# A fused attention and two expert layers: the reciprocal of the row sums taken before they are spread, and each group's value matmuls queued as one block

## The chip, the cores and the metric

The kernel runs on one core of one Trainium2 chip. The metric is the device time of one execution in microseconds (us); the figure for a kernel is the median of its timed runs. For the kernel before it is 1182.77 us over 3 runs, which lie between 1182.54 and 1185.65 us.

Five engines work side by side, each with its own in-order queue: TensorE (PE in the rows, with its weight loads as PEld), VectorE (DVE), ScalarE (ACT), GpSimd (POOL) and SyncE (SP, which here only issues DMAs).

## The reference, cut to what matters

```python
scores = scale * np.matmul(q_rot, k_rot.transpose(0, 1, 3, 2))      # B=2, H=8, S=576, D=64
scores = scores - np.max(scores, axis=-1, keepdims=True)
attn = np.exp(scores)
attn = attn / (np.sum(attn, axis=-1, keepdims=True) + 1e-09)
x = np.matmul(attn, v)                   # then laid out as (B*S, H*D) = (1152, 512)
x = ((x @ w1) * (x @ w2)) @ w3 @ w_out   # first layer, d_ff = 1024
P = sinkhorn(exp(x @ w_gate - max))      # 8 rounds over 1152 tokens x 8 experts
out = sum(P[:, e:e+1] * (np.maximum(x @ mw1[e], 0.0) @ mw2[e]) for e in range(8))
```

q and k are rotated before the scores (rotary embedding). Everything is float32.

## The kernel before, in words

The program has two stages. **Attention** comes first and is followed by the two matmul layers, which are not touched by the change (they begin with `branch`, L646, and end with `project`, L829).

Attention goes over 8 pairs of heads (`n`, two heads `j` per pair, 64 rows of the contraction each). The 576 queries of a pair are five tiles of 128 rows (the fifth, `MIX`, holds the last 64 queries of both heads), and the tiles form two groups (`TILES`): group 0 has tiles 0 and 1 (256 queries per head), group 1 has tiles 2, 3 and 4 (320 queries per head). Per tile and head:

- `scores` (L327, L340; `mixed_scores` L345, L363 for the fifth tile): matmuls into the PSUM tile `s`, two buffers.
- `row_max` (L370, VectorE) and `exponentials` (L374, ScalarE), which also leaves the row sum in one column of `sm`.
- `transposes` (L388, L391, L394, TensorE) of the exponentials `e` into the PSUM tile `t`, and `moved` (L407, VectorE or ScalarE) from there into `et0` or `et1`, which have one buffer each.

Per group:

- `norm_sums` (L411, ScalarE) adds 1e-9 to the 4 or 5 sums per row.
- `norm_rows` (L418, VectorE) takes the reciprocal of the sums, read 64 times each through a broadcast, so that it writes 128x256 or 128x320 elements into `rb`.
- `norm_columns` (L424, L427, TensorE) transposes `rb`; `norm_moved` (L432, ScalarE) copies the result out of PSUM into `r`.
- `values` (L440, TensorE): five parts `t` = 0 to 4, each a pair of matmuls of V against `et` that write the two 64-row halves of the PSUM tile `x` (one buffer, pool psX). One such matmul shows as two rows of the trace, so a group is 20 rows.
- `x_scale` (L448, VectorE) multiplies `x` with `r` into `xs` and frees `x`; `x_hi` (L459, ScalarE) and `x_lo` (L463, GpSimd or VectorE) split it into two parts.

Between these stand steps for the next layers: 24 weight units of 128x512 (`wide_steps` L565: L183, L188, L191, L196, L201, L204 on ScalarE, VectorE and GpSimd) and the product of two weight matrices (`w34_product`, L231 to L233, on TensorE). Rotating q and k of later pairs is on GpSimd (L272, L276, L292).

The order of all of it is worked out before the kernel is emitted by `Plan` (L52). Every step has a cost in us on its engine, a rank, the steps it needs, the buffers it takes and the buffers it frees. `Plan.order` moves a clock forward; whenever an engine is free it picks, of the steps that could start now, the one with the lowest rank. The order in which the steps are picked is the order in which they stand in the engines' queues. The plan assumes 0.36 us (256 elements) and 0.43 us (320 elements) for `norm_rows` by `on_dve`, and adds `TURN` = 0.1 us whenever TensorE goes from a `paired` step (`values`) to another or back:

```python
if e == "pe":
    d += self.TURN * (paired != was_paired)
    was_paired = paired
```

In the plan the value steps of group 0 have a rank of t + 23 and those of group 1 of t + 34 (t grows by 18 per pair): they come behind the scores of the next pair where both could start. Each of the five parts is a step of its own, so other TensorE work may be queued between two parts. Where the plan leaves TensorE idle early on, matmuls of an identity (L615) are put in to fill the time.

Of the kernel before, what the change touches and what calls it, by code (L numbers as in the profile page):

```python
# [18 lines left out]
P = 128  # L19
B, H, S, D = 2, 8, 576, 64  # L20
# [7 lines left out]
MID = NBLK // 2  # L28
SPAD = 640
NQ = NBLK // 2 + 1  # L30
MIX = NQ - 1
SF = 2 * P
HS = S // 2
G0, G1 = 256, S - 256
HD = P // 2
TILES = (0, 1), (2, 3, 4)
CN = 320, 256
# [83 lines left out]
def attention_two_moes(ctx: ExitStack, tc: tile.TileContext, rope, qk, v, mw12, mw3t, mwo, wg, ew1, ew2, out):  # L121
# [7 lines left out]
    pe, act, dve, pool, sp = nc.tensor, nc.scalar, nc.vector, nc.gpsimd, nc.sync  # L129
# [12 lines left out]
    def three(ps, terms):  # L142
# [15 lines left out]
    psS, psT, psX, psW = (  # L158
        aps.enter_context(tc.tile_pool(name=n, bufs=k, space=PSUM)) for n, k in (("psS", 2), ("psT", 2), ("psX", 1), ("psW", 1))
    )  # L160
# [89 lines left out]
    V = [att_p.tile([P, NBLK + 1, D], F32, name=f"v{i}") for i in range(2)]  # L250
# [7 lines left out]
    raw, K, st = {}, {}, {}  # L258
# [37 lines left out]
    def spread_q(n, j, x):  # L296
# [5 lines left out]
        else:  # L302
            sp.dma_start(dst[:, : MIX * P], src[:, : MIX * P])
            sp.dma_start(dst[:, MIX * P + HD :], src[:, MIX * P :])

# [7 lines left out]
    def half(j):  # L313
        return slice(j * D, (j + 1) * D)

    def group(i):

        return (0, i, i * P) if i < 2 else (1, i - 2, i * P - G0)
# [26 lines left out]
    def mixed_scores(n):  # L345
# [5 lines left out]
        for j in range(2):  # L351
# [6 lines left out]

            pieces = [(0, 0, 0, HS), (1, 0, HS, HS)] if j == 0 else [(0, 0, HD, HS), (1, 0, HD + HS, HS - HD), (1, HS - HD, 0, HD)]
            terms += [(q, k, pieces) for q, k in new]  # L360
# [18 lines left out]
    def transposes(n, i, part):  # L379
# [12 lines left out]
        if part:  # L392
            for j in range(2):
                pe.matmul(ps[half(j), 1, :HD], e[:, MID * P : S], ident[:, half(j)], start=True, stop=True)  # L394

    def moved(n, i, part, eng):
# [6 lines left out]
        else:  # L403
            b = (slice(0, 6), slice(6, 9))[part]
            dst = et[:, b, q0 : q0 + HD]
            src = st["t", n, i, part].rearrange("p t (j q) -> p (t j) q", j=2)[:, : b.stop - b.start]
# [5 lines left out]

    def norm_rows(n, g):

        k = 4 + g
        sm = st["sm", n, g][:, :k]
        st["rb", n, g] = rb = att_p.tile([P, 5, D], F32, name="rb", bufs=2)
        dve.reciprocal(rb[:, :k], sm.unsqueeze(2).to_broadcast([P, k, D]))  # L418

    def norm_columns(n, g):  # L420
        rb = st["rb", n, g]
# [3 lines left out]
        if g:  # L425
            for j in range(2):
                pe.matmul(ps[half(j), 2, :HD], rb[:, 4], ident[:, half(j)], start=True, stop=True)  # L427

# [2 lines left out]
        ng = (G0, G1)[g]  # L431
        act.copy(r[:, :ng], st["rt", n, g].rearrange("p i q -> p (i q)")[:, :ng])  # L432

    def values(n, g, t):

        ng = (G0, G1)[g]
        if t == 0:
            st["x", n, g] = psX.tile([P, DM], F32, name="x")
        for j in range(2):
            pe.matmul(  # L440
                st["x", n, g][half(j), :ng], V[n % 2][:, 2 * t + j], st["et", n, g][:, 2 * t + j * (t < MID)],
                start=(t == 0), stop=(t == MID),
            )

    def x_scale(n, g):
        ng = (G0, G1)[g]
# [20 lines left out]
    def step(f, args, costs, rank, needs=(), takes=(), frees=(), **kw):  # L467

        many = f in (rope_mul, rope_add, rope_lo, moved, x_lo)
        plan.step((f, *args), costs, rank, lambda e: f(*args, ENG[e]) if many else f(*args), needs, takes, frees, **kw)  # L470


    act_ps, act_sb = (lambda n: 0.12 + n / 1450), (lambda n: 0.1 + n / 1190)
    on_dve, on_pool, moving = (lambda n: 0.09 + n / 945), (lambda n: 0.1 + n / 440), (lambda n: n / 250e3)
# [6 lines left out]
    for n in range(NP):  # L481
        t = n * NQ * TILE
        step(load_v, (n,), {"sp": moving(4 * P * (NBLK + 1) * D)}, t - 40.0, takes=[("v", n)])
        ready = []
        for w in (1, 0):
            pieces = (every,) if n else halves if w else (slice(0, SF), slice(SF, S))
            for c in pieces:
                a, m = (n, w, c), c.stop - c.start
                r = t - 30.0 if n else -50.0 if c.start == 0 or w else -40.0
# [8 lines left out]
                fr = [("raw", (n, w))] if n == 0 and c is pieces[-1] else []  # L498
# [6 lines left out]
            for j, x in ((j, x) for j in range(2) for x in range(2)):  # L505
# [4 lines left out]
                else:  # L510
                    needs = [((rope_hi, rope_lo)[x], n, 0, every)]
# [3 lines left out]
        for i in range(NQ):  # L515
            g, k, _ = group(i)
            r = t + i * TILE
            for j in range(2 - (i == MIX)):
# [3 lines left out]
                fr = [("kk", n), ("sq", n)] if n and i == MIX else []  # L522
                needs = ready[0] + (ready[1] if n or i * P >= SF else ready[1][:1]) + before
# [3 lines left out]
                else:  # L527
                    made = mixed_scores, n
                    if n == 0:
                        for q in range(2):  # L530
                            step(mix_first, (q,), {"act": 0.2}, r, ready[1])
                        needs = needs + [(mix_first, 0), (mix_first, 1)]
# [3 lines left out]
                fr = [("psS", (n, i, j))] + [("nm", (n, i))] * (j or i == MIX)  # L536
                step(exponentials, (n, i, j), {"act": 0.73}, r, [(row_max, n, i, j)], frees=fr)
            r += TILE
            parts = 3 - (i == MIX)
            for p in range(parts):  # L540
                needs = [(exponentials, n, i, min(p, 1) * (i < MIX))] + ([(transposes, n, i, p - 1)] if p else [(transposes, n, i - 1, 0)] if k else [])
                tk = [("psT", (n, i, p))] + ([(f"et{g}", n)] if k == p == 0 else [])
                step(transposes, (n, i, p), {"pe": 0.33}, r, needs, tk, [("e", (n, i))] if p == parts - 1 else [])
                m = 3 * (P if i < MIX else P - HD * p)
                step(moved, (n, i, p), {"act": act_ps(m), "dve": on_dve(m)}, r, [(transposes, n, i, p)], frees=[("psT", (n, i, p))])
        for g, tiles in enumerate(TILES):
            a, ng = (n, g), (G0, G1)[g]
            r = t + (tiles[-1] + 2.0) * TILE
            needs = [(exponentials, n, i, j) for i in tiles for j in range(2 - (i == MIX))]
            step(norm_sums, a, {"act": 0.2}, r, needs)  # L550
            step(norm_rows, a, {"dve": on_dve((4 + g) * D)}, r, [(norm_sums, *a)], [("rb", a)], [("sm", a)])
            step(norm_columns, a, {"pe": (0.24, 0.4)[g]}, r, [(norm_rows, *a)], [("psT", (*a, "r"))], [("rb", a)])
            step(norm_moved, a, {"act": act_ps(ng)}, r, [(norm_columns, *a)], [("r", a)], [("psT", (*a, "r"))])
            r += 3.4 * TILE
            for m in range(MID + 1):
                parts = [(i, p) for i in tiles for p in (({0, 2}, {1})[m > 2] if i < MIX else {int(m > 2)})]
                needs = [(moved, n, i, p) for i, p in parts] + [(load_v, n)]
                needs += [(values, n, g, m - 1)] if m else []
                fr = [(f"et{g}", n)] + [("v", n)] * g if m == MID else []
                step(values, (n, g, m), {"pe": ng / 600}, r, needs, [("psX", a)] if m == 0 else [], fr, paired=True)  # L560
            step(x_scale, a, {"dve": on_dve(ng)}, r, [(values, n, g, MID), (norm_moved, *a)], [("xs", a)], [("psX", a), ("r", a)])
            step(x_hi, a, {"act": act_sb(ng)}, r, [(x_scale, *a)])
            step(x_lo, a, {"pool": on_pool(ng), "dve": on_dve(ng)}, r, [(x_hi, *a)], frees=[("xs", a)], port=both)

# [20 lines left out]
    for u in range(2 * KF):  # L585
        i = u // 2
# [3 lines left out]
        for j in range(4):  # L590
            needs = [(wo_load, u % 2 * 4 + j, 5), (w3_load, u, 5)]
# [169 lines left out]
    m = 14 * CN[1]  # L761
# [158 lines left out]
    for s in range(1, NSTEP):  # L920
        for c in range(2):
            for u in range(2):
# [3 lines left out]
                n = FT * (cut if u == 0 else len(done) - cut)  # L926
# [80 lines left out]
```

## Time and profile before

| | |
|---|---|
| median of 3 runs | 1182.77 us |
| the profiled execution's own time | 1184.76 us |
| its span | 1183.0 us |
| TensorE busy | 1144.8 us, 97% of the span |
| VectorE busy | 742.6 us, 63% |
| ScalarE busy | 423.0 us, 36% |
| GpSimd busy | 200.8 us, 17% |
| mean granted TensorE clock | 0.991 of full speed |

The span goes from the first to the last instruction; the execution's own time is 1.8 us longer. A clock of 1.00 is 2.4 GHz, 0.50 is 1.2 GHz. Busy shares are means over stages with different limits, so the shares of the table say little of attention alone.

### The profile page before, as it was taken

How to read it: one execution, taken by the hardware profiler on the slowest of the kernel's cores; microseconds unless marked ns; L12 is line 12 of the kernel's file. 1: busy time of each engine (PE TensorE's matmuls, PEld its weight loads, DVE VectorE, ACT ScalarE, POOL GpSimd, SP SyncE). 2: the span in 40 equal slices, each digit the busy share in tenths (PEclk: the TensorE clock that was granted, in tenths of full speed). 3: DMA queues.
4: the chain of work that ended last, by engine and by line, in shares of the span. 5: the costliest groups of instructions: out<-in, count | busy, mean ns of one | idle time of the engine just before them, and what ended most of it. 6: DMA issues, size and time to landing. Idle time of an engine off the chain costs nothing.

```text
span 1183.0 us, 17650 instructions
## 1 busy us (share of the span) xinstructions
PE 1144.8 (97%) x7058; PEld 1006.9 (85%) x7058; DVE 742.6 (63%) x1325; ACT 423.0 (36%) x900; POOL 200.8 (17%) x202
## 2 busy tenths in 40 slices
PE   9997998999999999999999999999999999999998
PEld 7675676678999988899898898989988989889887
DVE  7898787767533476656556566656565566665643
ACT  5675565534332333322323233222232323232311
POOL 3443462132100000211101111011021110101100
PEclk9998999999999999999999999999999999999999
DMA  6764565233100011111102111111021111110102
GB/s 209 211 220 147 173 164 139 89 96 119 54 19 19 5 51 36 54 54 36 55 18 72 37 36 55 52 38 54 19 72 37 36 54 41 50 53 20 36 9 71
DMA packets 29153, 83.07 MB, mean 70 GB/s; under 512 B 4880, under 2 KB 6416, under 8 KB 29072
## 3 DMA queue, kind: packets, MB, share of 16 engines
q1 hardware_dynamic: 28528, 81.36, 21.9%
q8 instruction: 55, 0.90, 0.3%
q10 hardware_dynamic: 544, 0.59, 0.2%
q14 instruction: 26, 0.21, 0.1%
HBM read 67.19 MB, written 2.36 MB: 59 GB/s over the span
## 4 chain that ended last, share of the span: by engine, by line
PE 83%; DVE 9%; DMA 3%; issue 2%; ACT 2%; POOL 1%; SPq 0%; ACTq 0%; DVEq 0%; POOLq 0%
PE z L838 11%; PE z L837 11%; PE z L839 11%; PE T L796 4%; PE T L797 4%; PE T L798 4%; PE Q L798 3%; PE Q L796 3%; PE Q L797 3%; PE A L798 3%; PE A L797 3%; PE A L796 3%; PE u L145 3%; PE u L147 3%; PE u L146 3%; PE x L440 2%
## 5 line engine op out<-in xcount | busy, mean ns | idle before, releaser
L839 PE MATMUL z<-w,h 128*128 128x512 f32 x576 | 226.3, 393 | 0.0
L846 DVE SCALAR_TENSOR_TENSOR acc<-z,pr,acc 128x512 f32<-128x512 f32 x135 | 101.0, 748 | 56.6 <-PE z L839 56.5
L839 PEld LDWEIGHTS z<-w,h 128*128 128x128 f32 x576 | 108.0, 187 | 25.3
L838 PE MATMUL z<-w,y 128*128 128x512 f32 x320 | 126.4, 395 | 0.0
L837 PE MATMUL z<-w,y 128*128 128x512 f32 x320 | 126.3, 395 | 0.0
L716 POOL TENSOR_TENSOR sums<-wide 128x256 f32<-128x256 f32 x28 | 22.8, 816 | 575.2 <-DMA wide<-in_ew_dram 340.2
L838 PE MATMUL z<-w,h 128*128 128x512 f32 x256 | 101.6, 397 | 0.0
L837 PE MATMUL z<-w,h 128*128 128x512 f32 x256 | 100.8, 394 | 0.0
L139 ACT CAST w<-wide 128x768 fp32r<-128x768 f32 (+1 forms) x64 | 60.3, 943 | 93.4 <-PE z L838 65.0
L140 DVE TENSOR_TENSOR w<-wide,w 128x768 fp32r<-128x768 f32 (+1 forms) x64 | 69.7, 1089 | 26.5 <-PE T L798 14.8
L802 ACT ACTIVATE y<-tmp 128x320 fp32r<-128x320 f32 x96 | 45.2, 470 | 113.8 <-DVE tmp L818 62.2
L802 ACT ACTIVATE h<-tmp 128x256 fp32r<-128x256 f32 x96 | 40.0, 416 | 127.5 <-DVE tmp L818 120.8
L145 PE MATMUL u<-x,w 128*128 128x320 f32 (+1 forms) x256 | 76.4, 298 | 3.8 <-DVE gf L658 2.6
L147 PE MATMUL u<-x,w 128*128 128x320 f32 (+1 forms) x256 | 75.7, 296 | 0.0
L146 PE MATMUL u<-x,w 128*128 128x320 f32 (+1 forms) x256 | 75.4, 295 | 0.0
L838 PEld LDWEIGHTS z<-w,y 128*128 128x128 f32 x320 | 60.7, 190 | 5.7
L837 PEld LDWEIGHTS z<-w,y 128*128 128x128 f32 x320 | 60.2, 188 | 6.0
L803 DVE SCALAR_TENSOR_TENSOR h<-tmp,y 128x320 fp32r<-128x320 f32 x96 | 47.5, 494 | 26.0 <-ACT y L802 25.8
L374 ACT ACTIVATE e<-s,nm 128x576 f32<-128x576 f32 x72 | 53.3, 742 | 25.8 <-DVE nm L370 25.4
L796 PE MATMUL T<-x,w 128*128 128x320 f32 x192 | 60.0, 312 | 0.1
L370 DVE TENSOR_REDUCE nm<-s 128x1 f32<-128x576 f32 x72 | 52.3, 745 | 11.8 <-PE s L340 9.6
L440 PE MATMUL x<-et,v 128*64 128x256 f32 (+1 forms) x320 | 50.9, 438 | 8.7 <-DVE xs L448 8.7
(224 smaller groups left out, 3042.6 us busy)
## 6 DMA issues: line engine op xcount, KB each, us to landing
wide<-in_ew_dram SPq DMA_DIRECT2D x64, 512.0 KB, 3.5
wide<-in_mw3t_dram SPq DMA_DIRECT2D x16, 512.0 KB, 4.2
wide<-in_mw_dram SPq DMA_DIRECT2D x16, 512.0 KB, 3.5
raw<-in_qk_dram SPq DMA_DIRECT2D x14, 576.0 KB, 5.1
kk<-raw SPq DMA_DIRECT2D x56, 144.0 KB, 2.5
wide<-in_mwo_dram SPq DMA_DIRECT2D x8, 512.0 KB, 6.5
v<-in_v_dram SPq DMA_DIRECT2D x8, 320.0 KB, 4.0
out_dram<-acc SPq DMA_DIRECT2D x8, 256.0 KB, 2.0
```

The costliest lines, as they stand in the source:

```text
L145: pe.matmul(ps, wh, xh, start=(i == 0), stop=False)
L146: pe.matmul(ps, wh, xl, start=False, stop=False)
L147: pe.matmul(ps, wl, xh, start=False, stop=(i == n - 1))
L440: pe.matmul(st["x", n, g][half(j), :ng], V[n % 2][:, 2 * t + j], st["et", n, g][:, 2 * t + j * (t < MID)], start=(t == 0), stop=(t == MID),)
L796: pe.matmul(ps, h[:, ws], x[0], start=(first and k == 0), stop=False, **kw)
L797: pe.matmul(ps, h[:, ws], x[1], start=False, stop=False, **kw)
L798: pe.matmul(ps, l[:, ws], x[0], start=False, stop=(k == 1), **kw)
L802: act.activation(h, src, AF.Relu)
L837: pe.matmul(ps, hh[:, f, ts], wh, start=(f == 0), stop=False)
L838: pe.matmul(ps, hh[:, f, ts], wl, start=False, stop=False)
L839: pe.matmul(ps, hl[:, f, ts], wh, start=False, stop=(f == FT - 1))
L846: dve.scalar_tensor_tensor(out=acc[t], in0=ps, scalar=p, in1=acc[t], op0=ALU.mult, op1=ALU.add)
```

## The change

`norm_rows` takes the reciprocal of the 4 or 5 sums in place. A new step, `norm_spread`, on ScalarE, copies each of them 64 times into `rb`. The five value parts become one (`VPARTS` has a single entry), so that the 20 rows of a group stand together in TensorE's queue, begin only when all moves of the group are done, and are one step of the plan.

```diff
+VPARTS = (0, 1, 2, 3, 4),
...
     def norm_rows(n, g):
+        sm = st["sm", n, g][:, : 4 + g]
+        dve.reciprocal(sm, sm)
+
+    def norm_spread(n, g):
         k = 4 + g
-        sm = st["sm", n, g][:, :k]
         st["rb", n, g] = rb = att_p.tile([P, 5, D], F32, name="rb", bufs=2)
-        dve.reciprocal(rb[:, :k], sm.unsqueeze(2).to_broadcast([P, k, D]))
+        act.copy(rb[:, :k], st["sm", n, g][:, :k].unsqueeze(2).to_broadcast([P, k, D]))
...
-    def values(n, g, t):
+    def values(n, g, part):
         ng = (G0, G1)[g]
-        if t == 0:
+        if part == 0:
             st["x", n, g] = psX.tile([P, DM], F32, name="x")
-        for j in range(2):
-            pe.matmul(...)
+        for t in VPARTS[part]:
+            for j in range(2):
+                pe.matmul(...)
...
-            step(norm_rows, a, {"dve": on_dve((4 + g) * D)}, r, [(norm_sums, *a)], [("rb", a)], [("sm", a)])
-            step(norm_columns, a, {"pe": (0.24, 0.4)[g]}, r, [(norm_rows, *a)], [("psT", (*a, "r"))], [("rb", a)])
+            step(norm_rows, a, {"dve": 0.12}, r, [(norm_sums, *a)])
+            step(norm_spread, a, {"act": act_sb((4 + g) * D)}, r, [(norm_rows, *a)], [("rb", a)], [("sm", a)])
+            step(norm_columns, a, {"pe": (0.24, 0.4)[g]}, r, [(norm_spread, *a)], [("psT", (*a, "r"))], [("rb", a)])
...
-            for m in range(MID + 1):
-                parts = [(i, p) for i in tiles for p in (({0, 2}, {1})[m > 2] if i < MIX else {int(m > 2)})]
-                needs = [(moved, n, i, p) for i, p in parts] + [(load_v, n)]
+            for m, blocks in enumerate(VPARTS):
+                parts = {(i, p) for i in tiles for t in blocks for p in (({0, 2}, {1})[t > 2] if i < MIX else {int(t > 2)})}
+                needs = [(moved, n, i, p) for i, p in sorted(parts)] + [(load_v, n)]
                 needs += [(values, n, g, m - 1)] if m else []
-                fr = [(f"et{g}", n)] + [("v", n)] * g if m == MID else []
-                step(values, (n, g, m), {"pe": ng / 600}, r, needs, [("psX", a)] if m == 0 else [], fr, paired=True)
+                last = m == len(VPARTS) - 1
+                fr = [(f"et{g}", n)] + [("v", n)] * g if last else []
+                step(values, (n, g, m), {"pe": len(blocks) * ng / 600}, r, needs, [("psX", a)] if m == 0 else [], fr, paired=True)
```

Since costs and steps of the plan change, the order of all steps of attention is worked out anew, on every engine.

## Rows read from the trace of the kernel before

**Rows 1.** Windows: us; busy us (x) of PE, PEld, DVE, ACT, POOL; clock; DMA; GB/s.

```profile
0.00:245.50 245.50, 217.10 (x1422) 161.88 (x1423) 194.77 (x273) 143.07 (x340) 91.42 (x65) 0.96 0.55 163
245.50:300.00 54.50, 50.74 (x355) 48.27 (x354) 40.52 (x66) 24.83 (x53) 19.73 (x14) 1.00 0.36 117
300.00:1183.00 883.00, 876.98 (x5286) 796.78 (x5284) 507.32 (x987) 255.07 (x507) 89.62 (x123) 1.00 0.13 42
```

**Rows 2.** Waits of TensorE in attention: us in total, times, longest us.

```profile
PE x L440 <- DVE xs L448: 8.7, 2, 5.9
PE t L424 <- DVE rb L418: 5.3, 7, 1.3
```

**Rows 3.** Chain of waits through attention: L418's pieces (start, us), first and last.

```profile
46.57 1.67 DVE rb L418
...
236.12 2.17 DVE rb L418
```

**Rows 4.** Groups by shape, VectorE's reciprocals in attention: count, busy us, mean ns, idle before.

```profile
L418 DVE RECIPROCAL rb<-sm 128x320 f32<-128x320 f32 x8 | 17.2, 2147 | 2.5 <-ACT sm L411 2.5
L418 DVE RECIPROCAL rb<-sm 128x256 f32<-128x256 f32 x8 | 14.0, 1747 | 0.7 <-ACT sm L411 0.7
```

**Rows 5.** One line's instructions, the gate's reciprocal of 8 elements: ns min/median/max.

```profile
L897 DVE RECIPROCAL cg<-cg x8: 192/199/204, 425.4 to 455.3; 128x8 f32<-128x8 f32 x8
```

**Rows 6.** Groups by shape, ScalarE's casts from one SBUF tile to another.

```profile
L459 ACT CAST x<-xs 128x320 fp32r<-128x320 f32 x8 | 3.7, 457 | 9.1 <-DVE xs L448 9.1
L459 ACT CAST x<-xs 128x256 fp32r<-128x256 f32 x8 | 3.3, 414 | 2.5 <-DVE xs L448 2.5
```

**Rows 7.** Timeline of VectorE and GpSimd ahead of TensorE's longest wait: start, us.

```profile
81.39 2.15 DVE L418 RECIPROCAL rb<-sm 128x320 f32<-128x320 f32 x1
83.85 0.69 DVE L191 SCALAR_TENSOR_TENSOR cvu<-wide,cvu 128x512 int32<-128x512 int32 x1
86.37 3.03 DVE L191 SCALAR_TENSOR_TENSOR cvu<-wide,cvu 128x512 int32<-128x512 int32 x1
91.12 3.09 DVE L196 SCALAR_TENSOR_TENSOR cvu<-cvy,cvu 128x512 int32<-128x512 int32 x1
94.81 0.41 DVE L448 TENSOR_TENSOR xs<-x,r 128x256 f32<-128x256 f32 x1
...
86.16 2.69 POOL L272 TENSOR_TENSOR raw<-raw,tab 128x1152 f32<-128x1152 f32 x1 [5.15 <-DMA raw<-in_qk_dram]
```

**Rows 8.** Timeline of TensorE, two value runs that waited, in brackets for what.

```profile
95.27 2.40 PE L440 MATMUL x<-et,v 128*64 128x320 f32 x8 [5.87 <-DVE xs L448]
...
125.20 0.76 PE L440 MATMUL x<-et,v 128*64 128x320 f32 x4 [2.88 <-DVE xs L448]
```

**Rows 9.** Timeline of TensorE: first and last value run, two others with what follows.

```profile
22.83 1.08 PE L440 MATMUL x<-et,v 128*64 128x256 f32 x8
...
103.74 0.76 PE L440 MATMUL x<-et,v 128*64 128x320 f32 x4
104.43 0.87 PE L388 MATMUL t<-ident,e 128*128 128x128 f32 x6
...
223.30 2.91 PE L440 MATMUL x<-et,v 128*64 128x320 f32 x20
226.15 0.50 PE L231 MATMUL t<-y 128*128 128x512 f32 x1
...
239.28 4.42 PE L440 MATMUL x<-et,v 128*64 128x320 f32 x20
```

**Rows 10.** Windows around the four stretches of attention with a clock below 1.

```profile
93.00:100.00 7.00, 4.73 (x22) 3.17 (x23) 4.34 (x6) 4.60 (x12) 0.67 (x1) 0.57 0.01 2
125.00:131.00 6.00, 5.80 (x29) 4.16 (x31) 4.86 (x7) 4.82 (x13) 4.94 (x4) 0.72 0.29 95
196.00:203.00 7.00, 5.22 (x25) 4.29 (x26) 4.91 (x7) 3.73 (x9) 0.00 (x0) 0.76 0.37 133
233.00:245.50 12.50, 8.65 (x46) 4.85 (x45) 4.62 (x6) 3.44 (x8) 0.26 (x1) 0.73 0.04 15
```

More of the change, by code (lines that the diff above doesn't have):

```diff
@@ L432, in norm_moved @@
         act.copy(r[:, :ng], st["rt", n, g].rearrange("p i q -> p (i q)")[:, :ng])
-    def values(n, g, t):
+    def values(n, g, part):
         ng = (G0, G1)[g]
-        if t == 0:
+        if part == 0:
             st["x", n, g] = psX.tile([P, DM], F32, name="x")
-        for j in range(2):
[L440 to L443, printed above, removed]
+        for t in VPARTS[part]:
+            for j in range(2):
+                pe.matmul(
+                    st["x", n, g][half(j), :ng], V[n % 2][:, 2 * t + j], st["et", n, g][:, 2 * t + j * (t < MID)],
+                    start=(t == 0), stop=(t == MID),
+                )
     def x_scale(n, g):
@@ L550, in attention_two_moes @@
             step(norm_sums, a, {"act": 0.2}, r, needs)
-            step(norm_rows, a, {"dve": on_dve((4 + g) * D)}, r, [(norm_sums, *a)], [("rb", a)], [("sm", a)])
-            step(norm_columns, a, {"pe": (0.24, 0.4)[g]}, r, [(norm_rows, *a)], [("psT", (*a, "r"))], [("rb", a)])
+            step(norm_rows, a, {"dve": 0.12}, r, [(norm_sums, *a)])
+            step(norm_spread, a, {"act": act_sb((4 + g) * D)}, r, [(norm_rows, *a)], [("rb", a)], [("sm", a)])
+            step(norm_columns, a, {"pe": (0.24, 0.4)[g]}, r, [(norm_spread, *a)], [("psT", (*a, "r"))], [("rb", a)])
             step(norm_moved, a, {"act": act_ps(ng)}, r, [(norm_columns, *a)], [("r", a)], [("psT", (*a, "r"))])
             r += 3.4 * TILE
-            for m in range(MID + 1):
-                parts = [(i, p) for i in tiles for p in (({0, 2}, {1})[m > 2] if i < MIX else {int(m > 2)})]
-                needs = [(moved, n, i, p) for i, p in parts] + [(load_v, n)]
+            for m, blocks in enumerate(VPARTS):
+                parts = {(i, p) for i in tiles for t in blocks for p in (({0, 2}, {1})[t > 2] if i < MIX else {int(t > 2)})}
+                needs = [(moved, n, i, p) for i, p in sorted(parts)] + [(load_v, n)]
                 needs += [(values, n, g, m - 1)] if m else []
-                fr = [(f"et{g}", n)] + [("v", n)] * g if m == MID else []
-                step(values, (n, g, m), {"pe": ng / 600}, r, needs, [("psX", a)] if m == 0 else [], fr, paired=True)
-            step(x_scale, a, {"dve": on_dve(ng)}, r, [(values, n, g, MID), (norm_moved, *a)], [("xs", a)], [("psX", a), ("r", a)])
+                last = m == len(VPARTS) - 1
+                fr = [(f"et{g}", n)] + [("v", n)] * g if last else []
+                step(values, (n, g, m), {"pe": len(blocks) * ng / 600}, r, needs, [("psX", a)] if m == 0 else [], fr, paired=True)
+            step(x_scale, a, {"dve": on_dve(ng)}, r, [(values, n, g, len(VPARTS) - 1), (norm_moved, *a)], [("xs", a)], [("psX", a), ("r", a)])
             step(x_hi, a, {"act": act_sb(ng)}, r, [(x_scale, *a)])
```

## The prediction

> **What bounds the kernel now.** I read the windows first, because the shares of the whole span hide where the time could move [rows 1]. From 300 us on TensorE is busy 876.98 of 883 us; nothing in the change reaches there, so that part only shifts. The same holds nearly for 245.5 to 300 us (50.74 of 54.5). The change lives in attention, the first 245.5 us. There TensorE is idle for 245.5 - 217.1 = 28.4 us, VectorE is busy for 194.77 us (79%) and ScalarE for 143.07 us (58%). No engine is full: TensorE and VectorE take turns in waiting for each other.
>
> The waits of TensorE come second [rows 2]: 8.7 us until an `xs` (the one PSUM tile `x` is freed late by `x_scale`), 5.3 us, in seven places, until an `rb`. Both are releases by VectorE. Third comes the chain of waits: nine of the sixteen reciprocals of L418 lie on it [rows 3], and their pieces add to 15.65 us. So VectorE's queue sets a good part of attention's length, and the reciprocals are its most conspicuous item: the plan gave them 0.36 and 0.43 us, the trace 1.75 and 2.15 us [rows 4].
>
> **The change part by part.** The sum is made against the profiled execution's own 1184.76 us, 2.0 us above the median of the runs.
>
> *Reciprocal.* From 256 to 320 elements the duration grows by 400 ns, 6.25 ns per element, with some 147 ns fixed [rows 4]. Four or five elements are then 0.17 to 0.18 us; the gate's reciprocal of 8 elements, at 0.199 us, lies on the same line [rows 5]. VectorE loses 8 x (1.747 - 0.172) + 8 x (2.147 - 0.178) = 28.4 us of work. What reaches the end is less. Of the nine pieces on the chain 15.65 us go and 9 x 0.175 = 1.6 us come back; in the four places where the next piece is TensorE's transpose of `rb`, ScalarE's copy and one more signal come in too (0.44 + 0.1 us each, 2.2 us). That is 11.9 us at most, if nothing is late right behind. Something is: the weight steps wait for their DMA and for GpSimd, and the maxima wait for TensorE. I take two thirds, -8 us, between 0 and -12. Below nothing I don't go for this part alone, since it takes away work.
>
> *The two long waits for `xs`.* Ahead of the 5.87 us one, VectorE's queue holds a reciprocal of 2.15 us, and operations of the weight steps that took 3.03 and 3.09 us where one takes 0.69, beside GpSimd's 2.69 us multiplication [rows 7, 8]. The reciprocal is already counted; the stretching stays or goes by how the new order happens to place the two engines. Ahead of the 2.88 us wait stands a reciprocal that the nine don't contain. I take -2 us, between +5 (two more such meetings at 2.4 us) and -8.7 (both waits gone).
>
> *Clock.* Four stretches of attention ran partly at 1.2 GHz, each behind or among waits: by the windows (1 - 0.67) x 7 + (1 - 0.72) x 6 + (1 - 0.76) x 7 + (1 - 0.73) x 12.5 = 9.0 us lost of full clock, of which TensorE was busy 24.4 of 32.5 us, so some 6.8 us of work [rows 10]. If one or two of the waits shrink, -2 us; between +2 and -6.8.
>
> *Value runs.* The 320 rows of L440 stand in 43 runs (24 of four rows, 10 of eight, 2 of twelve, 5 of sixteen, 2 of twenty), of which the first, the last and two others are shown [rows 9]. A run of four takes 104.43 - 103.74 = 0.69 us to the next instruction, one of twenty 226.15 - 223.30 = 2.85 us. So four more rows cost 0.54 us, and beginning and leaving a run costs 0.15 us. With sixteen runs, 27 x 0.15 = 4.05 us of TensorE go; at 88% busy I count -3.5 us, between 0 and -4.1.
>
> *ScalarE's copy.* The nearest rows are its casts between SBUF tiles of the same sizes, 0.414 and 0.457 us [rows 6]: 16 of them are 7.0 us. ScalarE is busy 58% of attention, so most of it lies in idle time; this cover is gone where the copy, queued ahead of exponentials, waits for a reciprocal that VectorE is late with. I take +1 us, between 0 and +7.
>
> *The block.* A group's first value rows can no longer go before its last move, and behind that move 2.85 us of value rows must run before `x` and `et` are free, where the last part alone took 0.69: 2.16 us later (for 256 queries somewhat less). Seven of sixteen groups already run sixteen or twenty rows in one go, so nine can pay: at most 9 x 2.16 = 19.4 us. Mostly the next pair's scores are queued ahead, and VectorE has work; I take +2 us, between 0 and +19.4. In the rows nothing passes a waiting value run: the 5.87 us run held all of TensorE [rows 8]. The Trainium skill, "TensorE: Matmul & The Clock Gate", Part 2, Step-by-step, states that matmuls stay in program order and only weight loads are pulled ahead; the trace agrees with its 5.87 us, and by that rule a block queued too early holds everything behind it, which is the last rival below.
>
> Sum: -8 - 2 - 2 - 3.5 + 1 + 2 = -12.5 us. The profiled execution would be 1172.3 us, the median 1182.8 - 12.5 = 1170.3, rounded to 1170. As a check from the other side: if attention scaled with VectorE's work it would lose 245.5 x (28.4 - 0) / 194.8 = 36 us, but TensorE needs its 217 us less the runs and the cold share, so some 206 us: no more than about 39 us are there in all.
>
> **The rivals.**
>
> *A, the forecast:* attention ends some 12 us earlier, 1170 us; its own range is 1160 to 1179.
>
> *B, hidden anyway:* VectorE's 28 us turn into idle time, as the chain goes over to the weight units' DMAs, TensorE and GpSimd. For it speaks that TensorE is 88% busy, against it the nine pieces on the chain. Only the runs and little else are gained: 1182.8 - 3.5 + 1 = 1180 us.
>
> *C, the order fits at last:* every group had put VectorE 1.4 to 1.7 us behind the plan, and lateness adds up in queues whose order is fixed. With right costs TensorE's idle time falls to a third: 28.4 us become 9.5, -18.9; clock -6; runs -4.1; copy and block, +3 in the sum, then lie in idle time, +0 to +1. That is -28 to -29, 1154 us. Against it: the other VectorE steps are longer than planned too.
>
> *D, slower:* the single buffers. The next pair's transposes need `et`, the next values need `x`; both are released at the end of the block. If all nine groups pay 2.16 us on the chain, +19.4; the reciprocals then bring half, -4, the runs -3.5, the copy +1, clock and `xs` waits nothing: +12.9, 1196 us. It outweighs the gains of the sum once seven of the nine pay in full (14.5 / 2.16 = 6.7).
>
> **How the numbers follow.** A 0.60, B 0.15, C 0.12, D 0.13. Two executions of this kernel can be told apart from about 0.3%, 3.5 us: faster is below 1179.2, slower above 1186.3. A and C lie below (0.72, less 0.02 of A's edge), and of B 0.07; D is above in 0.11 and inside in 0.02. So faster 0.77, same 0.12, slower 0.11. The range: C's far side at 1152 (30.8 us off, most of what TensorE's waits and cold stretches hold), and up to 1187, which takes in B, the upper bounds of copy or `xs` collisions and the weak half of D; 0.1 of D and some 0.06 below stay outside.
>
> **What would show it.** L418 as sixteen instructions of about 0.18 us; sixteen copies of 0.41 to 0.46 us on ScalarE; value rows in runs of twenty, the wait "PE t <- DVE rb" replaced by one on ScalarE and shorter than 5.3 us in sum; VectorE's busy time up to the end of attention 26 to 30 us lower; the first L145 some 12 us earlier, and the stretch behind it of unchanged length. It would be wrong if TensorE's idle time in attention stays near 28 us although VectorE's work is gone (B), if long waits for `xs` or `et` now stand before value blocks or transposes (D), or if the time behind attention changes.

## The result, and the profile after

The changed kernel takes 1167.01 us (median of 4 runs, 1161.74 to 1169.59) against 1182.72 us: a ratio of 0.9856, with a 95% interval of 0.9817 to 0.9894. The forecast was 1170 us. The profiled execution took 1168.12 us, 16.6 us less than that of the kernel before.

First the stretches that answer to [rows 1]: attention, the start of the branches, the rest (columns as there).

```profile
0.00:228.40 228.40, 210.98 (x1436) 165.34 (x1437) 170.17 (x273) 146.94 (x351) 100.10 (x71) 0.97 0.60 175
228.40:283.00 54.60, 50.63 (x354) 48.25 (x353) 40.78 (x66) 24.63 (x53) 19.76 (x14) 1.00 0.36 117
283.00:1165.90 882.90, 876.90 (x5285) 796.74 (x5283) 506.98 (x987) 255.21 (x507) 90.19 (x123) 1.00 0.13 42
```

The second and third stretch are as long as before (54.6 for 54.5, 882.9 for 883 us) and TensorE is as busy in them. All of the gain lies in attention: 17.1 us, of which 6.1 us are TensorE's busy time (217.1 to 211.0) and 11.0 us its idle time (28.4 to 17.4). VectorE's busy time fell by 24.6 us. TensorE's busy time holds the matmuls of an identity that the plan puts into its early gaps, and the new plan has more of them: 170 with 25.4 us in place of 156 with 22.2 us. So its other matmuls lost some 9 us.

The waits of TensorE in attention, which answer to [rows 2] (us in total, times, longest us):

```profile
PE t L389 <- ACT e L375: 5.0, 4, 2.1
PE t L392 <- ACT e L375: 3.0, 2, 2.5
...
PE t L429 <- ACT rb L423: 1.4, 1, 1.4
...
PE x L446 <- DVE xs L454: 0.3, 1, 0.3
```

The wait for `xs` is gone (8.7 to 0.3 us), that for `rb` has become one of 1.4 us and has moved from VectorE to ScalarE. What leads now are waits for exponentials, 8.0 of 17.1 us. In the chain of waits through attention the reciprocals had 6.5%; now none has a share that shows, and what leads is a transfer (before, then after):

```profile
by line: PE x L440 10.3%; PE s L340 8.1%; PE t L388 7.2%; DVE rb L418 6.5%; issue 5.8%; PE w L615 5.5%; DVE nm L370 5.2%; DVE cvu L191 4.8%; DVE cvu L196 4.7%; DMA wide<-in_mw3t_dram 3.7%; DVE cvu L188 3.2%; DMA wide<-in_mwo_dram 3.1%; DMA 
by line: DMA wide<-in_mw3t_dram 7.9%; PE x L446 7.7%; PE s L341 7.5%; issue 6.7%; PE t L389 6.0%; DMA raw<-in_qk_dram 4.4%; DVE nm L371 3.9%; ACT e L375 3.8%; DVE cvu L197 3.4%; DVE cvu L192 3.0%; DVE cvu L189 2.8%; PE w L232 2.8%; DMA kk<-
```

The new instructions, by shape (to be read beside [rows 4] and [rows 6]: count, busy us, mean ns, idle before), and the first and last of the sixteen value runs with one between (beside [rows 9]):

```profile
L417 DVE RECIPROCAL sm<-sm 128x5 f32<-128x5 f32 x8 | 1.5, 187 | 3.7 <-ACT sm L412 3.6
L417 DVE RECIPROCAL sm<-sm 128x4 f32<-128x4 f32 x8 | 1.4, 171 | 4.0 <-ACT sm L412 4.0
L423 ACT COPY rb<-sm 128x320 f32<-128x320 f32 x8 | 3.7, 459 | 1.7 <-DVE sm L417 1.6
L423 ACT COPY rb<-sm 128x256 f32<-128x256 f32 x8 | 3.3, 408 | 0.6 <-DVE sm L417 0.6
```

```profile
22.60 2.38 PE L446 MATMUL x<-et,v 128*64 128x256 f32 x20
...
81.69 4.50 PE L446 MATMUL x<-et,v 128*64 128x320 f32 x20
...
222.47 4.05 PE L446 MATMUL x<-et,v 128*64 128x320 f32 x20
```

The reciprocals went from 31.2 to 2.9 us; ScalarE's copies take 7.0 us and wait 2.2 us for them. Each value run has its 20 rows. The two long ones ran in part at 1.2 GHz: the windows with a clock below 1 are these, to be read beside [rows 10].

```profile
60.00:80.00 20.00, 17.26 (x129) 14.21 (x129) 14.22 (x26) 14.24 (x36) 13.19 (x9) 0.95 0.63 171
80.00:100.00 20.00, 19.28 (x121) 14.61 (x120) 15.11 (x24) 13.47 (x32) 9.10 (x6) 0.88 0.74 217
160.00:180.00 20.00, 17.54 (x102) 13.78 (x102) 17.09 (x27) 11.47 (x27) 8.29 (x5) 0.91 0.67 180
220.00:240.00 20.00, 17.79 (x105) 13.88 (x106) 10.09 (x18) 7.51 (x16) 5.54 (x4) 0.91 0.20 58
```

They lose (0.05 + 0.12 + 0.09 + 0.09) x 20 = 7.0 us of full clock, 2.0 us less than before. Both figures come from one execution each. Over the changed kernel's four executions here and the six of its repeat below, the mean clock goes from 0.994 to 0.999, some 6 us, so a difference of 2 us is not shown.

### The profile page after: what moved, and what is told of

Read it like the earlier page. It is cut to its first block, busy times and chain, and to the rows that moved or that the text cites. A ratio compares the mean times of both kernels' runs of the same rounds, so it can differ in the third digit from the quotient of the medians.

```text
span 1165.9 us, 17698 instructions
## 1 busy us (share of the span) xinstructions
PE 1138.5 (98%) x7072; PEld 1010.3 (87%) x7072; DVE 717.9 (62%) x1325; ACT 426.8 (37%) x910; POOL 210.0 (18%) x208
## 4 chain that ended last, share of the span: by engine, by line
PE 82%; DVE 7%; DMA 5%; issue 2%; ACT 2%; POOL 1%; SPq 1%; DVEq 0%; ACTq 0%; POOLq 0%
PE z L846 12%; PE z L845 11%; PE z L847 11%; PE T L804 4%; PE T L805 4%; PE T L806 4%; PE Q L806 3%; PE Q L804 3%; PE Q L805 3%; PE A L806 3%; PE A L805 3%; PE A L804 3%; PE u L146 3%; PE u L147 3%; PE u L148 3%
## 5 line engine op out<-in xcount | busy, mean ns | idle before, releaser
L724 POOL TENSOR_TENSOR sums<-wide 128x256 f32<-128x256 f32 x28 | 23.5, 838 | 574.8 <-DVE w L141 296.8
L804 PE MATMUL T<-x,w 128*128 128x320 f32 x192 | 59.9, 312 | 0.1
L805 PE MATMUL T<-x,w 128*128 128x320 f32 x192 | 59.2, 309 | 0.0
L806 PE MATMUL T<-x,w 128*128 128x320 f32 x192 | 59.1, 308 | 0.0
```

The lines of the kernel that those rows point to most:

```text
L804: pe.matmul(ps, h[:, ws], x[0], start=(first and k == 0), stop=False, **kw)
L805: pe.matmul(ps, h[:, ws], x[1], start=False, stop=False, **kw)
L806: pe.matmul(ps, l[:, ws], x[0], start=False, stop=(k == 1), **kw)
```

## The experiments

Theory T: the work taken off VectorE carries most of the gain and the block of values only the few us that fewer runs save. Its rivals: the order of the queues, made anew by the plan, carries it (O); the two parts only pay together (S); the block costs (D). The first two expectations have O and S in one rival, R: the blocks, or the order that came with them, carry the gain. Ratios are to the kernel before, run beside each, with 95% intervals.

**Each part alone, planned anew.** The reciprocal alone keeps the value parts as five steps:

```diff
-VPARTS = (0, 1, 2, 3, 4),
+VPARTS = (0,), (1,), (2,), (3,), (4,)
```

> The short reciprocal and ScalarE's spread alone; the value matmuls stay in five parts that the plan places one by one, as before. Theory T (VectorE's removed work carries most of the gain, the block the 4 us of TensorE that its fewer runs save): 1169 to 1174 us, TensorE's idle time in attention as short as in the changed kernel (about 17 us), value rows in about 40 runs. Rival R (the blocks, or the order of queues that came out with them, carry the gain): 1178 to 1183 us.

Measured: 1178.54 us, ratio 0.9974 (0.9957 to 0.9991), only 3.7 us. The block alone keeps the 64-fold reciprocal, its cost in the plan included:

```diff
-        dve.reciprocal(sm, sm)
...
-        act.copy(rb[:, :k], st["sm", n, g][:, :k].unsqueeze(2).to_broadcast([P, k, D]))
+        dve.reciprocal(rb[:, :k], sm.unsqueeze(2).to_broadcast([P, k, D]))
...
-            step(norm_rows, a, {"dve": 0.12}, r, [(norm_sums, *a)])
-            step(norm_spread, a, {"act": act_sb((4 + g) * D)}, r, [(norm_rows, *a)], [("rb", a)], [("sm", a)])
+            step(norm_rows, a, {"dve": on_dve((4 + g) * D)}, r, [(norm_sums, *a)], [("rb", a)], [("sm", a)])
```

> The long 64-fold reciprocal on VectorE as before; only the five value parts become one step. T: sixteen runs instead of 43 save about 4 us of TensorE, VectorE is as loaded as before: 1177 to 1181 us. Rival R: 1167 to 1172 us. Rival D (blocks cost, and the shorter reciprocal pays for it): 1184 us or more.

Measured: 1176.7 us, ratio 0.9959 (0.9943 to 0.9976), 5.5 us. So 3.7 and 5.5 us make 15.7 together. Read naively that is S: the reciprocal alone misses T's 1169 to 1174 us and lies in R's range, the block alone lies 0.3 us under T's range and far above R's. But each of these kernels also has an order of its own in every queue, so the parts must be tried in one order.

**The reciprocal in fixed orders.** In the order of before, with the short reciprocal and the copy issued where the long one stood:

```diff
-        dve.reciprocal(rb[:, :k], sm.unsqueeze(2).to_broadcast([P, k, D]))
+        dve.reciprocal(sm, sm); act.copy(rb[:, :k], sm.unsqueeze(2).to_broadcast([P, k, D]))
```

> The plan and the order of every queue are those of the kernel before; where the long reciprocal stood, the short one is issued and ScalarE's copy of 64-fold right with it. T: the work taken off VectorE shortens attention without any new order, by 8 to 14 us: 1169 to 1175 us. Rival O (the gain is that of an order made anew with costs that fit): 1179 us or more, since ScalarE's queue now has a copy at a place that the plan did not choose.

Measured: 1173.75 us, ratio 0.9935 (0.9915 to 0.9956), 8.5 us. In the order of the changed kernel, from the other side, once with VectorE's work put back where nothing waits for its result, and once with the long reciprocal itself:

```diff
         dve.reciprocal(sm, sm)
+        idle = att_p.tile([P, 4, D], F32, name="idle")
+        dve.reciprocal(idle, sm[:, :4].unsqueeze(2).to_broadcast([P, 4, D]))
```

> The changed kernel, in its own order, with a reciprocal of 256 elements into an unused tile added behind each short one: 16 x 1.75 = 28 us of VectorE work come back, and nothing waits for their result. T: most of the reciprocals' share returns, 8 to 14 us on the changed kernel: 1175 to 1181 us. Rival O: VectorE's load is not what matters, 1167 to 1171 us.

```diff
-        sm = st["sm", n, g][:, : 4 + g]
-        dve.reciprocal(sm, sm)
+        k = 4 + g
+        st["rb", n, g] = rb = att_p.tile([P, 5, D], F32, name="rb", bufs=2)
+        dve.reciprocal(rb[:, :k], st["sm", n, g][:, :k].unsqueeze(2).to_broadcast([P, k, D]))
     def norm_spread(n, g):
-        ...
-        act.copy(rb[:, :k], st["sm", n, g][:, :k].unsqueeze(2).to_broadcast([P, k, D]))
+        pass
```

> Every queue in the order of the changed kernel, but norm_rows writes the 64-fold reciprocal as before, and ScalarE copies nothing. Theory T (taking the reciprocals off VectorE is worth 6 to 9 us in whichever order the queues stand): 1173 to 1179 us, 6 to 10 us above the changed kernel. Rival S (reciprocal and block only pay together, as alone they gave 3 and 5 us and together 16): 1180 us or more.

> The changed kernel once more, as the yardstick for the three beside it: 1163 to 1170 us.

Measured: 1172.92 us with the idle reciprocals (ratio 0.9923, 0.9898 to 0.9947), 1175.51 us with the long ones (0.9945, 0.9927 to 0.9963), and 1166.46 us for the changed kernel beside the latter (0.9856, 0.983 to 0.9882). The reciprocal is thus worth 8.5 us in the old order and 1175.51 - 1166.46 = 9.1 us in the new one (7.7 and 10.5 us by the ratios): for the reciprocal that is T, and neither S nor O. The other 6.3 us, by which the long form in the new order lies under the kernel before (1181.84 us beside it), belong to the new order with its blocks; that is more than T's 4 us. The 28.0 us of VectorE work that nothing waits for cost 6.5 us against that repeat (7.9 by the ratios). Another 2.6 us may come with the longer way to `rb`, but the intervals of the two kernels overlap, so that is not shown. T's span for the idle load, 1175 to 1181 us, was too high by 2 us. The trace of the long form in the new order, in attention's window and the waits, and the waits with the idle reciprocals (its profiled execution, 1177.73 us, is the slowest of six):

```profile
0.00:234.99 234.99, 209.94 (x1431) 164.22 (x1431) 186.53 (x272) 140.73 (x334) 98.06 (x71) 0.99 0.59 170
```

```profile
PE t L389 <- ACT e L375: 7.4, 5, 4.5
PE t L428 <- DVE rb L418: 4.6, 3, 2.9
```

```profile
PE t L389 <- ACT e L375: 7.1, 5, 3.0
PE t L392 <- ACT e L375: 2.9, 2, 2.5
PE s L341 <- ACT e L375: 2.9, 4, 1.3
```

With the long form TensorE is idle for 25.1 us again, and the waits for `rb` by VectorE are back at 4.6 us. Its waits for exponentials, all lines together, are 9.9 us, hardly more than the 8.0 and 9.3 us of the changed kernel's two traces. With the idle reciprocals they are 12.9 us; that is where the load by itself shows, as the maxima ahead of the exponentials stand in VectorE's queue.

**The block in the old order.** All five parts are issued where the last of them stood; everything else keeps its place. With long and with short reciprocals:

```diff
     def values(n, g, t):
         ng = (G0, G1)[g]
-        if t == 0:
-            st["x", n, g] = psX.tile([P, DM], F32, name="x")
-        for j in range(2):
-            pe.matmul(...)
+        if t < MID:
+            return
+        st["x", n, g] = psX.tile([P, DM], F32, name="x")
+        for t in range(MID + 1):
+          for j in range(2):
+            pe.matmul(...)
```

> The order of the kernel before, long reciprocals too; but a group's five value parts are all issued where the last of them stood. T (block = saved runs): 27 runs of 0.15 us go from TensorE, 2 to 4 us: 1178 to 1181 us. Rival D (the block holds x and et longer, up to 2.16 us per group): 1184 us or more. Rival N (the block of the change gained through the new order, not through its runs): within 1.5 us of the kernel before.

> The order of the kernel before with both changes in it: short reciprocal with ScalarE's copy right behind, and value parts issued where the last of them stood. T: both gains add, 8 and 3 us: 1169 to 1173 us. Rival S (they only pay together): 1166 us or less. Rival O (the new order is worth the rest): 1173 us or more, 6 us above the changed kernel.

Measured: 1194.6 us, ratio 1.0116 (1.0095 to 1.0137), with the long reciprocals: 12.8 us slower. With the short ones 1182.19 us, ratio 1.0003 (0.9988 to 1.0019), 8.4 us above the same kernel without gathering (1173.75 us). T is wrong for both, and D is right here: a block in the wrong place costs more than its runs save. (The second also lies in O's range, 1173 us or more.) The waits of TensorE in attention, before, and gathered with long reciprocals:

```profile
PE s L340 <- ACT e L374: 2.6, 3, 2.1
PE t L391 <- ACT e L374: 2.2, 1, 2.2
...
PE t L388 <- ACT e L374: 1.3, 3, 0.8
```

```profile
PE t L388 <- ACT e L374: 9.7, 8, 4.6
PE t L424 <- DVE rb L418: 7.1, 6, 1.8
PE s L340 <- ACT e L374: 5.4, 5, 2.3
...
PE t L391 <- ACT e L374: 2.5, 2, 2.3
```

And TensorE's timeline around one of its holes, before and gathered, and around another, gathered (start us, us, in brackets the wait):

```profile
46.49 1.08 PE L440 MATMUL x<-et,v 128*64 128x256 f32 x8
48.37 0.41 PE L424 MATMUL t<-ident,rb 128*128 128x128 f32 x2 [0.80 <-DVE rb L418]
```

```profile
47.08 0.49 PE L388 MATMUL t<-ident,e 128*128 128x128 f32 x3
49.41 0.41 PE L424 MATMUL t<-ident,rb 128*128 128x128 f32 x2 [1.84 <-DVE rb L418]
...
65.09 0.77 PE L340 MATMUL s<-kk,sq 128*128 128x288 f32 x4
70.18 0.90 PE L388 MATMUL t<-ident,e 128*128 128x128 f32 x3 [4.33 <-DVE et L407]
```

The kernel before waited 0.80 us at the first of these places, because eight value rows of 1.08 us stood there. The single parts had been filling TensorE's waits. Gathered, they leave the holes, and then mostly stand as 2.3 to 2.9 us ahead of transposes and of scores whose maxima and exponentials come later for it. The waits for `e` rose from 6.1 to 17.6 us in sum (the transposes of L388 from 1.3 to 9.7 us); with short reciprocals they are 17.6 us too, against 5.7 us in the same order without gathering, so this is the gathering's price and not the reciprocal's. The waits for `xs` are gone, which gives 8.7 us back. The clock's mean in attention fell from 0.96 to 0.95. The second hole is of another kind: no value rows stood there before either, where TensorE waited 1.53 us. It is longer mainly because the move it waits for stands behind two operations of the weight steps that met GpSimd's (see the last section) and took 1.78 and 2.91 us; in the kernel before they took 0.69 and 2.94 us.

**Split or block, each in an order of its own.** So is the block's gain in the changed kernel the luck of one order? Ranks spaced by 3.55 or 3.65 in place of 3.6 make all queues anew with the same work (but for the number of identity matmuls, 166 to 184 in these four, 170 and 174 in the two at 3.6):

```diff
-    TILE = 3.6
+    TILE = 3.55
```

> The changed kernel with ranks spaced by TILE = 3.55 instead of 3.6, which makes the order of all queues anew with the same work and the same costs. Theory B (blocks planned as one step give the better order, whatever the spacing): 1163 to 1172 us and at least 4 us under the split kernel of the same spacing. Rival L (1178.5 against 1166.5 us was the luck of one order): 1172 us or more, or within 2 us of the split one.

> Short reciprocal and ScalarE's copy, value parts planned one by one, TILE = 3.55. B: 1174 to 1182 us, at least 4 us above the block kernel of the same spacing. L: within 2 us of it, or below.

> The changed kernel with TILE = 3.65. B: 1163 to 1172 us and at least 4 us under the split kernel of the same spacing. L: 1172 us or more, or within 2 us of the split one.

> Short reciprocal and ScalarE's copy, value parts planned one by one, TILE = 3.65. B: 1174 to 1182 us, at least 4 us above the block kernel of the same spacing. L: within 2 us of it, or below.

| TILE | five parts | one block | difference |
|---|---|---|---|
| 3.55 | 1178.53 us, 0.9978 (0.9958 to 0.9997) | 1165.28 us, 0.9868 (0.9835 to 0.9901) | 13.3 us |
| 3.6 | 1178.54 us, 0.9974 (0.9957 to 0.9991) | 1166.46 us, 0.9856 (0.983 to 0.9882) | 12.1 us (13.9 by the ratios) |
| 3.65 | 1167.43 us, 0.9881 (0.9865 to 0.9897) | 1161.97 us, 0.9826 (0.9806 to 0.9846) | 5.5 us |

The block is ahead at all three, by at least the 4 us that its theory asked for, so it isn't luck; its size is: five parts spread over 11 us by the spacing alone, blocks over 4.5 us. (The two kernels at 3.6 were not run beside each other. For five parts at 3.65 the expected 1174 to 1182 us were missed by 7 us.) The block at 3.65 has the lowest median of all; against the changed kernel the intervals overlap, so that those 4.5 us are likely rather than shown. The windows of attention: five parts and block at 3.65.

```profile
0.00:228.91 228.91, 211.43 (x1428) 158.62 (x1428) 173.38 (x282) 144.82 (x346) 92.13 (x65) 0.99 0.60 175
```

```profile
0.00:221.96 221.96, 205.80 (x1446) 163.48 (x1446) 162.27 (x264) 149.36 (x357) 99.61 (x72) 0.99 0.61 180
```

At this spacing the block wins 5.6 us of TensorE's busy time and 1.3 us of idle time. At 3.6 the same pair of windows, cut like these where the matmuls behind attention begin, gives 212.6 to 209.8 us busy and 23.5 to 17.4 us idle; with the trace of the repeat it is 207.2 us busy and 19.4 us idle, so a profiled pair is good to some 2 us.

## Why the prediction was right, point by point

- *What bounds the kernel:* right. Attention alone changed, and the waits for `rb` and `xs` were those that went.
- *Reciprocal:* 0.178 and 0.172 us were forecast, 0.187 and 0.171 us measured; 28.4 us of VectorE's work, 28.3 measured; -8 us at the end, -8.5 and -9.1 us in fixed orders. That VectorE's busy time fell by less than 26 to 30 us has other reasons: operations beside it took longer, L197 for example 1077 ns in place of 943 (3.5 us in all), and the new order gives VectorE 47 of the large moves in place of 42 (2.9 us).
- *Waits for `xs`:* -2 us was too little. Nearly all of the 8.7 us went, but not by the reciprocal alone: in the old order with short reciprocals 5.6 us of them are still there. Either other part of the change removes them: no value run waits for `xs` with five parts planned anew at 3.6, and none in the old order with gathered parts and long reciprocals.

```profile
PE x L440 <- DVE xs L448: 5.6, 2, 3.6
```

- *Clock:* -2 us, which the windows have too (9.0 to 7.0 us of full clock), but executions of one kernel differ by more: not shown.
- *Value runs and block:* this is the term that was mis-sized. -3.5 and +2 us were put side by side, as if the block stood in the same order. In the old order it costs 12.8 us, runs included, where the last rival's terms for block and runs alone would give 19.4 - 3.5 = 15.9 us. And it comes through unfilled holes and late exponentials (11.5 us more of such waits) rather than through `x` held longer, as no wait for `xs` is left. Planned as one step it is worth 5.5 us with long reciprocals and 5.5 to 13.3 us with short ones, by the spacing. TensorE's matmuls keep their order, as the Trainium skill has it ("TensorE: Matmul & The Clock Gate", Part 2, Step-by-step); the traces agree: while the transposes at 102.45 us of the gathered kernel waited 4.55 us, TensorE ran no other matmul. The runs add that the price of a block is set by what the plan puts around it.
- *ScalarE's copy:* 0.414 and 0.457 us were taken from casts, 0.408 and 0.459 us measured. ScalarE waits 2.2 us for the reciprocal, TensorE 1.4 us for the copy, which fits the +1 us.
- *The rivals:* B is out, as the fixed orders show. C said that an order made with costs that fit is better: with five parts that hangs on the spacing, 1178.54 us made anew at 3.6 and 1167.43 us at 3.65 against 1173.75 us in the old order. D is real but not in this change.
- *Luck:* the sum has no term for the order made anew. As that alone moves five parts by 11 us, the forecast's 12.5 us against the measured 15.7 us are closer than its working could promise.

What stays open is why the plan makes better orders of blocks. TensorE's busy time falls by 2.8 us at 3.6 (212.6 to 209.8), in which its fewer runs and a lower clock (0.97 against 0.99) stand together, and the 6.1 us of idle time that went with them no run traces to one step of the plan. Only one wait goes with the block at all three spacings: that of the weight product (L232) for `keep`, 1.8, 1.6 and 1.9 us with five parts. Those for the moves into `et` fall at 3.55 (8.0 to 0.9 us) and 3.6 (4.3 to 2.1 us) and rise at 3.65 (3.0 to 5.0 us).

## What to carry to other kernels

Where a queue's order is written ahead, measure a change of the work in a fixed order (the old one and the new one), and a change of the order at several settings of the planner: two of these splits differ by 11 us with the same work for the task. Don't let an engine compute the same value 64 times: take the costly operation on the few elements and let an engine with idle time spread them. Small independent matmuls that fill another chain's waits can be worth more where they stand than the switches they cost, as here in the old order, unless something else is planned into the holes.

## What the runs showed of the hardware

ScalarE reads each of 4 or 5 elements 64 times over at the price of a plain cast of the output's size: 0.408 and 0.459 us, where the casts of [rows 6] took 0.414 and 0.457 us. VectorE's reciprocal, by contrast, pays for each element that it writes, however few it reads: 1747 ns for 256 from 4 [rows 4], 171 ns for 4.

A VectorE operation on two SBUF inputs that meets a GpSimd operation in these traces doesn't slow down beside it, it waits for it. In the gathered kernel, VectorE's and then GpSimd's rows:

```profile
95.28 3.16 DVE L204 TENSOR_TENSOR y<-cvu,y 128x512 fp32r<-128x512 f32 x1
98.37 1.88 DVE L196 SCALAR_TENSOR_TENSOR cvu<-cvy,cvu 128x512 int32<-128x512 int32 x1
```

```profile
94.95 2.95 POOL L272 TENSOR_TENSOR raw<-raw,tab 128x1152 f32<-128x1152 f32 x1 [5.64 <-DMA raw<-in_qk_dram]
97.98 1.73 POOL L276 TENSOR_TENSOR raw<-raw 128x576 f32<-128x576 f32 x1
```

The first ends 0.54 us after GpSimd's operation that began before it (98.44 against 97.90 us), the second 0.54 us after the next (100.25 against 99.71 us). The Trainium skill ("SBUF — State Buffer", SBUF: two separate sides) calls the pair of ports that the two engines share an exclusive lock, held for a whole instruction; the trace agrees. In the first 260 us of the kernels before and after, all eighteen such operations on 128x512 elements that took more than 1 us (0.69 us otherwise) end 0.54 to 0.56 us after a GpSimd operation that had begun before them. Behind these two operations stood a maximum, and TensorE waited 4.55 us for its exponential, the longest wait of that kernel. The longest of the kernel before, 5.87 us, came of three such meetings: the two of [rows 7, 8] and, between them, one of 1.88 us (L204 at 89.32 us).
